# One attention and maxout FFN kernel: a new issue order, whole-row weight loads and two-bank folds

## The chip, the cores and the metric

The kernel runs on one core of a Trainium2 chip. The metric is device time in microseconds of one execution. The core has five engines that run side by side, each through its own queue in program order: TensorE (PE in the rows; its weight loads are PEld), VectorE (DVE), ScalarE (ACT), GpSimd (POOL) and SyncE (SP). POOL and SP issue the DMAs here. Engines wait for each other through semaphores.

## The reference

```python
a = softmax(phi)                       # over the 32 memory slots
k_m = einsum('bhsm,bhsd->bhmd', a, k)  # per head: 32 x 64
v_m = einsum('bhsm,bhsd->bhmd', a, v)
attn = softmax(q @ k_m.T / 8)          # 576 x 32 per head
x = attn @ v_m                         # heads side by side: 4608 x 512
h = maximum(maximum(x @ w1, x @ w2), x @ w3)   # 4608 x 768
out = h @ w_out                        # 4608 x 512, f32
```

Batch 8, heads 8, sequence 576, head size 64, 32 memory slots, d_ff 768. All inputs and the output are f32 in HBM; the loads cast to bf16, except phi.

## The kernel before

All heads of a batch are handled at once, in pairs of heads on 128 partitions. The program multiplies v_m into the weights instead of forming x: for each batch it makes "folded" weights v_m w1, v_m w2 and so on, and multiplies attn by those. The maximum over three is rewritten: with w1 and w2 replaced by w1 - w3 and w2 - w3 (w_diff, line 160), h is relu and max of two projections plus x w3, and the w3 part goes straight to the output through w3 w_out (made once by w3_t, line 137, and w3_o, line 148).

Work per batch b is cut into steps with letters (the table in issue, line 435). L loads phi, k, v and q. E is exp(phi) on ScalarE. B is k_m and v_m, 72 small matmuls into kvp. N normalizes on VectorE. K transposes k_m and v_m and VectorE copies them to kv and vk. Q0, Q1, Q2 transpose q, VectorE copies to qT. S0, S1 are the scores, then their exponentials on ScalarE (e2). M0, M1 are the sums over slots by a matmul with block ones and then, on ScalarE, logarithm and exponential, giving the reciprocal r. X0, X1 multiply e2 by r on VectorE into attn. D0, D1, D2 fold the weights, D3 folds w3 w_out; ScalarE evacuates even folds (line 344), VectorE odd ones (line 346). F0 to F11 are the projections: even ones end in a relu on ScalarE (h1, line 371), the odd one after it in a max with that h1 on VectorE (line 373) into hT. T0 to T3 are output tiles of 128 rows: six matmuls with w_out and two with the folded w3 part, a copy on ScalarE (line 417), and a store of two tiles on the SP queue. T4, of every second batch, is one more tile with the leftover 64 rows of two batches.

The order of all this is written out by hand as text (lines 461 to 485): each engine gets its instructions in the order in which the steps are issued. A plus or minus after a step's name means a later or an earlier batch. Batches 2 to 6 run in a loop, one pass each; a pass holds F and T of batch b, tiles T2, T3, T4 of batch b - 1, S to D of b + 1, B, N, K, Q and the loads further ahead.

PSUM is held as three buffers of two banks with the tag acc (kvp, sc, sm, wps, acc take turns) and two of one bank with the tag one (pt, kvt, po). A step waits until the reader of the tile three (or two) allocations earlier is done. phi, q, k and v have two buffers each, so loads run two batches ahead. All loads are issued by POOL, in program order: batch 0 in two halves, the weights in six pieces and w_out, then batch 1. Before the first data arrives, warm_up issues 16 matmuls on zeros.

Of the kernel before, what the change touches and what calls it, by code (L numbers as in the profile page):

```python
# [15 lines left out]
def kernel(  # L16
# [303 lines left out]
    def fold(b, n):  # L320

        s = st[b]
        W = BANK // 2
# [14 lines left out]
        if n < 3:  # L338
            out_ = wps[b][:, :, n].rearrange("p g i f -> p g (i f)")
        else:  # L340
            wp3s[b] = quad.tile([P, NG, DM], BF16, name="wp3")
            out_ = wp3s[b]
        if n % 2 == 0:
            nc.scalar.copy(out=out_, in_=ps)  # L344
        else:
            nc.vector.tensor_copy(out=out_, in_=ps)  # L346
# [35 lines left out]
    def ffn2(b, t):  # L382
# [31 lines left out]
        if t < 4:  # L414
            if t == 0:
                osts[b] = work.tile([P, 4, DM], FP32, name="ost")
            nc.scalar.copy(out=osts[b][:, t], in_=po)  # L417
            if t % 2 == 1:
# [14 lines left out]


    def issue(b, n):

        if not 0 <= b < B or (n == "T4" and b % 2 == 0):
# [14 lines left out]
            "T": lambda: ffn2(b, i),
        }[n[0]]()

    def run(b, text):

        for w in text.split():
            n = w.rstrip("+-")
            issue(b + w.count("+") - w.count("-"), n)

    warm_up(16)
    for h in range(2):
        att_exp(0, slice(2 * h, 2 * h + 2))
    for h in range(2):
        att_kv(0, range(2 * h, 2 * h + 2))
    run(0, "N Q0 Q1 Q2 L++ K S0 S1 M0 M1")
    w3_t(0)
    run(0, "X0 X1")
    w3_t(1)
    w3_t(2)  # L470
    for j in range(NP):
        w3_o(j)
    w_diff(0)
    run(0, "D0 D3 F0 F1 F2 F3")
    w_diff(1)
    run(0, "D1 F4 F5 E+")
    w_diff(2)
    run(0, "F6 F7 D2 F8 F9 F10 F11 T0 T1 B+ N+ T2 Q0+ Q1+ Q2+ K+ L+++ S0+ S1+")
# [37 lines left out]
```

## Time and profile before

| what | us |
|---|---|
| time before, median of 3 runs (218.95 to 221.14) | 220.83 |
| the profiled execution, its own time | 221.6 |
| span of that profile, first to last instruction | 219.8 |
| TensorE busy, VectorE busy, ScalarE busy, GpSimd busy | 182.0, 101.2, 107.2, 32.0 |
| mean granted clock of TensorE, as a share of full | 0.910 |

An engine's busy time is the sum of its instructions' records; a TensorE record includes its pipeline, so records of neighbours overlap, and the distance between two starts tells better what a step costs there. Idle time before an instruction is put down to the engine that released it. The span starts with the first instruction; the time of a run is some 2 us longer than the span.

### The profile page before, as it was taken

What the parts mean: (1) busy time and instruction counts of PE and PEld (TensorE: products, weight loads), DVE (VectorE), ACT (ScalarE), POOL (GpSimd) and SP (SyncE); (2) the same over time, 40 slices, a digit from 0 to 9 for tenths busy, and PEclk for the clock granted to TensorE, in tenths of its full rate; (3) what the DMA queues carried; (4) which work ended last, traced back from release to release, by engine and by line L of the source; (5) the groups of instructions that cost most, each with busy time, mean ns of one, the idle gap of its engine ahead of it and who ended that gap; (6) DMA issues with size and microseconds to landing.
All of it is one profiled execution on the core that took longest, in us unless ns stands there. A gap on an engine that the chain in (4) does not pass through costs nothing.

```text
span 219.8 us, 4458 instructions
## 1 busy us (share of the span) xinstructions
PE 182.0 (83%) x1912; PEld 100.7 (46%) x1912; DVE 101.2 (46%) x169; ACT 107.2 (49%) x178; POOL 32.0 (15%) x48
## 2 busy tenths in 40 slices
PE   7547896669787996499799988988998899899991
PEld 2234533335424743256345654564456445545540
DVE  6214705441608651942664295265525752552500
ACT  3102435343168439358265855674658259554431
POOL 8933230010401214120111110000000000000000
PEclk9855579679966999889999999999999999999998
DMA  4999999994796897999985994331033024113335
GB/s 99 187 204 207 202 262 208 263 207 137 136 210 170 179 206 160 232 219 207 211 175 160 142 204 74 98 98 35 13 98 95 4 47 102 57 37 95 98 95 143
DMA packets 23092, 31.75 MB, mean 144 GB/s; under 512 B 1312, under 2 KB 17440, under 8 KB 23072
## 3 DMA queue, kind: packets, MB, share of 16 engines
q0 software_dynamic: 17824, 22.02, 55.9%
q1 hardware_dynamic: 5248, 9.44, 16.1%
q8 instruction: 15, 0.25, 0.4%
q14 instruction: 5, 0.04, 0.1%
HBM read 39.32 MB, written 9.44 MB: 222 GB/s over the span
## 4 chain that ended last, share of the span: by engine, by line
PE 50%; ACT 19%; DVE 18%; issue 5%; DMA 5%; POOL 2%; ACTq 0%; DVEq 0%; POOLq 0%
PE po L388 19%; PE acc L361 13%; PE po L397 6%; DVE hT L373 6%; DMA qq<-in_q_dram 5%; ACT h L371 4%; ACT ln L300 4%; PE po L151 3%; PE wps L330 3%; ACT r L306 3%; DVE qT L241 3%; ACT ost L417 3%; ACT e L278 3%; DVE attn L311 3%; ACT wp L344 2%
## 5 line engine op out<-in xcount | busy, mean ns | idle before, releaser
L361 PE MATMUL acc<-attn,wp 128*128 128x288 bf16 x384 | 61.1, 304 | 5.5 <-ACT wp L344 1.7
L373 DVE TENSOR_TENSOR hT<-acc,h 128x576 bf16<-128x576 f32 x48 | 36.3, 756 | 48.3 <-ACT h L371 28.1
L388 PE MATMUL po<-wo_sb,hT 128*128 128x512 bf16 x216 | 55.1, 387 | 4.1 <-DVE hT L373 2.3
L361 PEld LDWEIGHTS <-wp 128*128 128x128 bf16 x384 | 38.2, 103 | 24.4 <-issue 6.2
L371 ACT ACTIVATE h<-acc 128x576 bf16<-128x576 f32 x48 | 30.6, 649 | 25.9 <-PE acc L361 25.7
L417 ACT COPY ost<-po 128x512 f32<-128x512 f32 x32 | 18.9, 590 | 41.4 <-PE po L397 41.4
L388 PEld LDWEIGHTS <-hT 128*128 128x128 bf16 x216 | 20.4, 99 | 30.8 <-issue 6.7
L346 DVE CAST wp<-wps 128x1024 bf16<-128x1024 f32 x16 | 19.1, 1221 | 19.6 <-PE wps L330 19.5
L397 PE MATMUL po<-wp,attn 128*128 128x512 bf16 x64 | 19.5, 387 | 0.0
L344 ACT CAST wp<-wps 128x1024 bf16<-128x1024 f32 x16 | 16.2, 1015 | 1.1 <-PE wps L330 1.1
L278 ACT ACTIVATE e<-sc 128x320 bf16<-128x320 f32 (+1 forms) x32 | 10.6, 425 | 12.6 <-PE sc L268 12.6
L311 DVE TENSOR_TENSOR attn<-e,r 128x576 bf16<-128x576 bf16 x16 | 12.0, 754 | 9.1 <-ACT r L306 9.0
L191 PE MATMUL kvp<-kvo,e 64*32 64x192 bf16 x576 | 9.7, 255 | 5.4 <-DMA kvo<-in_v_dram 4.5
L330 PE MATMUL wps<-w_sb,vk 64*32 64x512 bf16 x96 | 9.0, 391 | 5.3 <-DVE w_sb L164 3.0
L180 ACT ACTIVATE e<-ph 128x1152 bf16<-128x1152 f32 (+1 forms) x9 | 9.5, 1056 | 7.4 <-DMA ph<-in_phi_dram 7.4
L241 DVE COPY qT<-pt 128x1024 bf16<-128x1024 bf16 x16 | 10.8, 685 | 3.1 <-PE pt L238 2.9
L87 POOL DMA_DIRECT2D ph<-in_phi_dram x9 | 6.9, 762 | 36.5 <-ACT e L180 32.7
L191 PEld LDWEIGHTS <-e 64*32 64x32 bf16 x576 | 8.2, 94 | 7.1 <-issue 6.8
L238 PE MATMUL pt<-ident,qq 128*128 128x128 bf16 x128 | 10.3, 231 | 1.4 <-DMA qq<-in_q_dram 1.1
L306 ACT ACTIVATE r<-ln 128x576 f32<-128x576 f32 x16 | 10.9, 683 | 0.5
L300 ACT ACTIVATE ln<-sm 128x576 f32<-128x576 f32 x16 | 10.4, 650 | 0.1
L204 DVE RECIPROCAL rden<-kvp 128x2 f32<-128x2 f32 x8 | 1.3, 168 | 19.8 <-PE kvp L191 19.8
(50 smaller groups left out, 151.6 us busy)
## 6 DMA issues: line engine op xcount, KB each, us to landing
out_dram<-ost SPq DMA_DIRECT2D x32, 256.0 KB, 3.3
qq<-in_q_dram POOLq DMA_DIRECT2D x8, 576.0 KB, 9.3
ph<-in_phi_dram POOLq DMA_DIRECT2D x7, 576.0 KB, 9.2
kvo<-in_k_dram POOLq DMA_DIRECT2D x7, 576.0 KB, 8.6
kvo<-in_v_dram POOLq DMA_DIRECT2D x7, 576.0 KB, 11.3
w_sb<-in_moe_w_dram POOLq DMA_DIRECT2D x3, 512.0 KB, 17.7
out_dram<-ot SPq DMA_DIRECT2D x8, 128.0 KB, 2.4
w_sb<-in_moe_w_dram POOLq DMA_DIRECT2D x3, 256.0 KB, 16.3
```

What stands on the lines that cost most here:

```text
L191: nc.tensor.matmul(kvp[M * j : M * (j + 1), a, 0 : 3 * D], lhsT=s["e"][r, j, c, :], rhs=kv[r, :, j, c, :], start=(c == 0), stop=(c == NC - 1),
L300: nc.scalar.activation(out=ln.rearrange("p (h n) -> p h n", h=2), in_=sm[:, :, 0:SH], func=AF.Ln,)
L306: nc.scalar.activation(out=r, in_=ln, func=AF.Exp, scale=-1.0)
L311: nc.vector.tensor_tensor(out=attns[b // 2][:, g, (b % 2) * S : (b % 2 + 1) * S], in0=s["e2"][:, g, 0:S], in1=s["r", g], op=ALU.mult,)
L344: nc.scalar.copy(out=out_, in_=ps)
L346: nc.vector.tensor_copy(out=out_, in_=ps)
L361: nc.tensor.matmul(acc[:, h, 0:SH], lhsT=wps[b][:, g, ft // 2, w, (ft % 2) * P : (ft % 2 + 1) * P], rhs=attn[:, g, c0 : c0 + SH], start=(g ...
L371: nc.scalar.activation(out=s["h1"], in_=a, func=AF.Relu)
L373: nc.vector.tensor_tensor(out=hT[:, ft, (b % 2) * S : (b % 2 + 1) * S].rearrange("p (h n) -> p h n", h=2), in0=a, in1=s["h1"], op=ALU.max,)
L388: nc.tensor.matmul(po, lhsT=hT[:, fc, c0 : c0 + P], rhs=wo_sb[:, fc, :], start=(fc == 0), stop=False,)
L397: nc.tensor.matmul(po, lhsT=attn[:, g, c0 : c0 + P], rhs=wp3s[b][:, g, :], start=False, stop=(g == NG - 1),)
L417: nc.scalar.copy(out=osts[b][:, t], in_=po)
```

## The change

- The hand-written order is replaced by another, from the first load to the last tile. The prologue (batches 0 and 1 and the start of 2 and 3) is one list of steps with batch numbers; the loop text and the last batch's text are new. F's are no longer issued in pairs, output tiles no longer in the order 0 to 3, and D0 to D3 no longer side by side.
- Loads are split by tensor: load_ph, load_kv and load_q. In the main part each is issued as soon as its buffer's last reader has been issued (done), not all four after K. The first phi goes out on the SP queue, in two halves.
- w1, w2 and w3 come by one load each instead of two. w1 and w2 are treated as one row of 1536 columns (w12) and folded in three pieces of 512; w_diff works on the same pieces.
- The evacuations of D are ScalarE, VectorE, ScalarE, ScalarE (D3 was VectorE's), those of T are VectorE for T0, T1, T2 and T4 and ScalarE for T3 (all were ScalarE's).
- M is split: M issues the matmuls, R the logarithm and exponential.
- The warm-up is 28, 9 and 7 matmuls, at three places.

```diff
-    def load(b, parts=1):
+    def load_ph(b):
         ph = inp.tile([P, NP, NC, M], FP32, name="ph")
+        loaded.setdefault(b, {})["ph"] = ph
+        dst = ph.rearrange("p j c m -> p j (c m)")
+        if b == 0:
+            for h in halves:
+                nc.sync.dma_start(out=dst[:, h], in_=by_pair(phi, b)[:, h])
+        else:
+            nc.gpsimd.dma_start(out=dst, in_=by_pair(phi, b))
...
-    def load_w(i, cols):
+    def load_w(i):
         w = (moe_w1, moe_w2, moe_w3)[i]
         nc.gpsimd.dma_start(
-            out=w_sb[:, :, i, cols], in_=w.rearrange("(j p) f -> p j f", p=P)[:, :, cols]
+            out=w_sb[:, :, i], in_=w.rearrange("(j p) f -> p j f", p=P)
         )
 
-    load(0, 2)
+    load_ph(0)
+    load_kv(0)
+    load_q(0)
     ident = const.tile([P, P], BF16, name="ident")
     make_identity(nc, ident)
-    third = DF // 3
-    part = [slice(0, third), slice(third, DF)]
-    for h in range(2):
-        load_w(2, part[h])
+    load_w(2)
     nc.gpsimd.dma_start(out=wo_sb, in_=moe_w_out.rearrange("(t p) c -> p t c", p=P))
-    for h in range(2):
-        for i in range(2):
-            load_w(i, part[h])
-    load(1)
+    load_w(0)
+    load_w(1)
+    load_ph(1)
+    load_kv(1)
+    load_q(1)
...
+    EVAC = {"D": "avaa", "T": "vvvav"}
+
+    def evacuate(kind, n, out_, in_):
+        if EVAC[kind][n] == "a":
+            nc.scalar.copy(out=out_, in_=in_)
+        else:
+            nc.vector.tensor_copy(out=out_, in_=in_)
...
+    w12 = w_sb[:, :, 0:2].rearrange("p j i f -> p j (i f)")
+
     def w_diff(n):
 
-        c = slice(n * third, (n + 1) * third)
-        for i in range(2):
+        c = n * BANK
+        while c < (n + 1) * BANK:
+            e = min((n + 1) * BANK, (c // DF + 1) * DF)
             nc.vector.tensor_tensor(
-                out=w_sb[:, :, i, c],
-                in0=w_sb[:, :, i, c],
-                in1=w_sb[:, :, 2, c],
+                out=w12[:, :, c:e],
+                in0=w12[:, :, c:e],
+                in1=w_sb[:, :, 2, c % DF : c % DF + e - c],
                 op=ALU.subtract,
             )
+            c = e
...
-                    rhs=w_sb[r, j, 0:2, n * W : (n + 1) * W] if n < 3 else w3o[r, j, :],
+                    rhs=w12[r, j, n * BANK : (n + 1) * BANK] if n < 3 else w3o[r, j, :],
...
-                    lhsT=wps[b][:, g, ft // 2, w, (ft % 2) * P : (ft % 2 + 1) * P],
+                    lhsT=wps[b][:, g, w * DF + ft * P : w * DF + (ft + 1) * P],
...
+    issued = set()
+    loads = ((load_ph, "E"), (load_kv, "B"), (load_q, "Q0 Q1 Q2"))
...
+    def done(b, n):
+        issued.add((b, n))
+        for f, names in loads:
+            names = names.split()
+            if n in names and b + 2 < B and all((b, m) in issued for m in names):
+                f(b + 2)
...
+    issue(0, "Z28")
+    att_exp(0, halves[0])
+    att_exp(0, halves[1])
+    done(0, "E")
+    att_kv(0, range(0, NP // 2))
+    issue(0, "Z9")
+    att_kv(0, range(NP // 2, NP))
+    done(0, "B")
+    run(0, "N Z7 Q0 Q1 Q2 K S0 S1 W0 M0 R0 M1 R1")
+    for w in """
+        W1@0 W2@0 V0@0 O1@0 X1@0 X0@0 O2@0 O3@0 D0@0 V1@0 O0@0 V2@0 F2@0 D1@0
+        F0@0 D2@0 F10@0 F1@0 D3@0 F4@0 F3@0 E@1 F11@0 F8@0 F5@0 B@1 N@1 F9@0
+        K@1 F6@0 Q0@1 D3@1 Q2@1 F7@0 Q1@1 E@2 T1@0 S0@1 S1@1 D1@1 T0@0 M1@1
+        R1@1 T3@0 B@2 D0@1 M0@1 N@2 K@2 R0@1 Q0@2 D2@1 X0@1 D0@2 X1@1 E@3
+        D1@2 T2@0 F6@1 F0@1 Q1@2 F1@1 F10@1 F4@1 D3@2 F7@1 F2@1 Q2@2 F11@1 F5@1
+        F8@1 F3@1 S0@2 B@3 N@3 D2@2 S1@2 Q0@3 M0@2 Q2@3 R0@2 F9@1 Q1@3 M1@2
+        X0@2 T0@1 R1@2 X1@2 T1@1 K@3 E@4
+    """.split():
+        n, b = w.split("@")
+        issue(int(b), n)
     for b in range(2, B - 1):
-        run(b, "F0 F1 T2- S0+ S1+ B++ D0+ T3- N++ F2 M0+ F3 M1+ F4 X0+ F5 Q0++ X1+ F6 Q1++ F7 Q2++")
-        run(b, "T4- F8 F9 K++ L++++ F10 F11 E+++ T0 D1+ D2+ D3+ T1")
-    run(B - 1, "F0 F1 T2- F2 F3 F4 T3- F5 F6 F7 T4- F8 F9 F10 F11 T0 T1 T2 T3 T4")
+        run(b, "F0 F6 F1 F8 F4 F7 F2 F5 F10 F3 F9 T2- S0+ D1+ S1+ T3- Q0++ M0+ R0+")
+        run(b, "M1+ F11 Q1++ T0 R1+ T4- Q2++ E+++ D0+ X0+ B++ D3+ X1+ N++ D2+ T1 K++")
+    run(B - 1, "F0 F2 F3 F8 F1 T2- F10 F9 F4 T4- F6 F5 F11 F7 T3- T2 T4 T1 T0 T3")
```

W stands for w3_t, O for w3_o, V for w_diff, Z for warm_up.

## Rows read from the trace of the kernel before

**Rows 1.** The page: busy us, share of the span and count of each engine

```profile
PE 182.0 (83%) x1912; PEld 100.7 (46%) x1912; DVE 101.2 (46%) x169; ACT 107.2 (49%) x178; POOL 32.0 (15%) x48
```

**Rows 2.** Stage table: window, length, busy PE, PEld, DVE, ACT, POOL, clock, DMA, GB/s

```profile
0.00:45.00 45.00, 31.05 (x234) 16.61 (x234) 19.41 (x33) 13.43 (x21) 17.87 (x29) 0.73 1.12 204
...
92.50:116.10 23.60, 21.22 (x243) 11.94 (x239) 12.76 (x22) 12.59 (x21) 4.35 (x6) 0.95 1.06 208
116.10:135.80 19.70, 17.95 (x228) 10.56 (x226) 11.07 (x20) 12.50 (x21) 2.22 (x3) 1.00 0.81 148
135.80:158.10 22.30, 19.92 (x237) 11.36 (x236) 11.29 (x20) 13.08 (x22) 0.00 (x0) 1.00 0.25 60
...
178.00:196.60 18.60, 17.56 (x144) 9.05 (x143) 8.20 (x11) 11.91 (x21) 0.00 (x0) 1.00 0.30 72
196.60:219.80 23.20, 18.61 (x107) 9.93 (x105) 4.87 (x7) 8.39 (x14) 0.00 (x0) 0.96 0.41 102
```

**Rows 3.** Timeline, batch 3's pass and end of 6's: start, us, engine, line, tiles

```profile
118.75 0.32 PE L268 MATMUL sc<-qT,kv 64*32 64x320 bf16 x4
...
119.69 0.09 PEld L330 LDWEIGHTS <-vk 64*32 64x32 bf16 x1
...
122.67 0.41 PE L292 MATMUL sm<-e,blkones 128*128 128x288 bf16 x2
122.92 0.65 PE L361 MATMUL acc<-attn,wp 128*128 128x288 bf16 x4
123.68 0.76 DVE L373 TENSOR_TENSOR hT<-acc,h 128x576 bf16<-128x576 f32 x1 [2.84 <-PE acc L361]
...
125.09 0.61 PE L238 MATMUL pt<-ident,qq 128*128 128x128 bf16 x8
125.54 0.65 PE L361 MATMUL acc<-attn,wp 128*128 128x288 bf16 x4
...
133.28 0.39 PE L330 MATMUL wps<-w_sb,vk 64*32 64x512 bf16 x1
...
134.05 1.47 PE L388 MATMUL po<-wo_sb,hT 128*128 128x512 bf16 x6
135.79 1.14 PE L361 MATMUL acc<-attn,wp 128*128 128x288 bf16 x8
136.77 1.46 PE L388 MATMUL po<-wo_sb,hT 128*128 128x512 bf16 x6
...
188.21 1.46 PE L388 MATMUL po<-wo_sb,hT 128*128 128x512 bf16 x6
...
190.15 0.54 PE L361 MATMUL acc<-attn,wp 128*128 128x288 bf16 x3
```

**Rows 4.** The page's costliest groups: busy, mean ns, idle before and its releaser

```profile
L373 DVE TENSOR_TENSOR hT<-acc,h 128x576 bf16<-128x576 f32 x48 | 36.3, 756 | 48.3 <-ACT h L371 28.1
...
L371 ACT ACTIVATE h<-acc 128x576 bf16<-128x576 f32 x48 | 30.6, 649 | 25.9 <-PE acc L361 25.7
L417 ACT COPY ost<-po 128x512 f32<-128x512 f32 x32 | 18.9, 590 | 41.4 <-PE po L397 41.4
...
L346 DVE CAST wp<-wps 128x1024 bf16<-128x1024 f32 x16 | 19.1, 1221 | 19.6 <-PE wps L330 19.5
...
L344 ACT CAST wp<-wps 128x1024 bf16<-128x1024 f32 x16 | 16.2, 1015 | 1.1 <-PE wps L330 1.1
```

**Rows 5.** POOL's load issues in time; last, landing times of the q loads

```profile
24.55 0.74 POOL L87 DMA_DIRECT2D qq<-in_q_dram  x1 [3.07 <-DMA wo_sb<-in_moe_w_out_dram]
...
29.76 0.74 POOL L87 DMA_DIRECT2D kvo<-in_v_dram  x1 [1.53 <-DMA w_sb<-in_moe_w_dram]
32.57 0.74 POOL L87 DMA_DIRECT2D qq<-in_q_dram  x1 [2.07 <-DMA w_sb<-in_moe_w_dram]
...
DMA to landing us min/median/max: 6.1/9.3/19.3
```

**Rows 6.** Timeline of VectorE: the last difference of weights

```profile
43.87 1.28 DVE L164 TENSOR_TENSOR w_sb<-w_sb 128x1024 bf16<-128x1024 bf16 x2
```

More of the change, by code (lines that the diff above doesn't have):

```diff
@@ new lines, in load_kv, with load_q @@
+    def load_kv(b):
+        kv = kvos[b % 2]
+        loaded.setdefault(b, {})["kv"] = kv
+        for h in halves if b == 0 else [slice(0, NP)]:
+            for i, src in enumerate((k, v)):
+                nc.gpsimd.dma_start(
+                    out=kv[:, i].rearrange("p j c d -> p j (c d)")[:, h],
+                    in_=by_pair(src, b)[:, h],
+                )
+    def load_q(b):
+        qq = inp.tile([P, NP, NC, D], BF16, name="qq")
+        loaded.setdefault(b, {})["q"] = qq
+        nc.gpsimd.dma_start(
+            out=qq.rearrange("p j c d -> p j (c d)"), in_=by_pair(q, b)
+        )
@@ L229, in att_q @@
         qq = loaded[b]["q"]
-        if jj == 0:
+        if "qT" not in s:
             s["qT"] = work.tile([P, NP, NCP, P], BF16, name="qT")
@@ L257, in att_score @@
         x = b % 2
-        if g == 0:
+        if "e2" not in s:
             s["e2"] = work.tile([P, NG, S + HP], BF16, name="e2")
@@ L322, in fold @@
         s = st[b]
-        W = BANK // 2
-        if n == 0:
-            wps[b] = work.tile([P, NG, 3, 2, W], BF16, name="wp")
+        if n == 3:
+            wp3s[b] = quad.tile([P, NG, DM], BF16, name="wp3")
+        elif b not in wps:
+            wps[b] = work.tile([P, NG, 2 * DF], BF16, name="wp")
         ps = acc_pool.tile([P, NG, BANK], FP32, name="wps", tag="acc")
@@ L337, in fold @@
                 )
[L338 to L346, printed above, removed]
+        evacuate(
+            "D", n, wp3s[b] if n == 3 else wps[b][:, :, n * BANK : (n + 1) * BANK], ps
+        )
     hts = {}
@@ L353, in ffn1 @@
         ft, w = n // 2, n % 2
-        if n == 0 and b % 2 == 0:
+        if b // 2 not in hts:
             hts[b // 2] = work.tile([P, FT, 2 * S], BF16, name="hT")
@@ L369, in ffn1 @@
         if w == 0:
-            s["h1"] = quad.tile([P, 2, SH], BF16, name="h1")
-            nc.scalar.activation(out=s["h1"], in_=a, func=AF.Relu)
+            h1 = s["h1", ft] = quad.tile([P, 2, SH], BF16, name="h1")
+            nc.scalar.activation(out=h1, in_=a, func=AF.Relu)
         else:
@@ L414, in ffn2 @@
         if t < 4:
[L415 to L418, printed above, removed]
+            if b not in osts:
+                osts[b] = work.tile([P, 4, DM], FP32, name="ost"), set()
+            ost, done = osts[b]
+            evacuate("T", t, ost[:, t], po)
+            done.add(t)
+            t0 = t - t % 2
+            if {t0, t0 + 1} <= done:
                 rows = out[b * S : (b + 1) * S, :].rearrange("(p c) d -> p c d", c=NC)
                 for u in range(2):
-                    c0 = 2 * (t - 1) + (u + b) % 2
+                    c0 = 2 * t0 + (u + b) % 2
                     nc.sync.dma_start(
                         out=rows[:, c0 : c0 + 3 : 2, :],
-                        in_=osts[b][HP * u : HP * (u + 1), t - 1 : t + 1],
+                        in_=ost[HP * u : HP * (u + 1), t0 : t0 + 2],
                     )
@@ L427, in ffn2 @@
             ot = work.tile([P, DM], FP32, name="ot")
-            nc.scalar.copy(out=ot, in_=po)
+            evacuate("T", t, ot, po)
             for u in range(2):
@@ L440, in issue @@
         {
-            "L": lambda: load(b),
             "E": lambda: att_exp(b),
@@ L459, in run @@
[L459 to L478, printed above, removed]
@@ L479 @@
-    run(0, "T3 D0+ M0+ M1+ D1+ X0+ X1+ D2+ D3+ E++")
-    run(1, "F0 F1 F2 F3 B+ F4 F5 N+ F6 F7 Q0+ F8 Q1+ F9 Q2+ K+ L+++ F10 F11 T0")
-    run(1, "S0+ S1+ E++ D0+ T1 M0+ M1+ X0+ X1+ B++ D1+ D2+ N++ Q0++ Q1++ Q2++ K++ L++++ D3+ E+++")
+            issue(b + w.count("+") - w.count("-"), w.rstrip("+-"))
+    issue(0, "Z28")
[6 more added lines that the diff above has]
+    done(0, "B")
```

33 lines of the change are left out of this document (16 added, 17 removed).

## The prediction, made before the changed kernel was run

> **What bounds the kernel now.** I read the page's busy shares first, then a table by stage, then the instructions of one loop pass in order of time, then the load queue at the start. The shares say TensorE is busy 83% of the span, ScalarE 49%, VectorE 46% [rows 1]. That 83% overstates TensorE: its records overlap, so I use distances between starts. The stage table cuts the span at the first projection (F0) of each pass: 92.5 us until batch 2's pass begins, then 23.6, 19.7, 22.3, 19.9 and 18.6 us for the passes of batches 2 to 6 (the longer ones, those of even batches, carry a T4 output tile; the last has no B, K, Q or E left), and 23.2 us of tail [rows 2] (the pass of batch 5 is left out there, it repeats batch 3's). [...]
>
> What must TensorE spend on a pass at full clock? From starts [rows 3]: S and B together 0.94 (118.75 to 119.69), M 0.25, Q 0.45, three D 0.77, T 1.74 (134.05 to 135.79), F 0.49 (two in 0.98), T4 1.94. So 12 F 5.88 + 4 T 6.96 + S and B 0.94 + 4 D 1.1 + 2 M 0.5 + Q 1.2 + K 0.1 = 16.7 us, with T4 18.6. The passes take 19.7 and 22.3: **3.0 to 3.7 us of each pass are stalls**, and no engine is the bound. In the pass of batch 3 ScalarE is busy 12.5 us (6 h of 0.649, 4 tile evacuations of 0.59, two folds of 1.015, the rest exponentials and logarithms), VectorE 11.1 [rows 2, 4]. The stalls are waits in a fixed order with three PSUM buffers for acc: late in the pass D1, D2, D3 come back to back, ScalarE evacuates T's that the next h waits behind, and F's come in pairs of one ScalarE and one VectorE user, so each VectorE max waits for its own h.
>
> At the start the bound is loads and an order. DMA share is 1.12 over the first 45 us, above full by the way it is counted (overlapping packets) [rows 2]. The last weight half has landed at 32.57, when the queue's next issue is released by it; q of batch 1 is issued at 24.55 and the longest landing of a q load is 19.3 us, so it is there by about 43.9; q of batch 2, issued at 32.57, by 51.9 [rows 5]. But the third difference of weights runs only at 43.87, behind two VectorE max operations [rows 6], 11 us after its data.
>
> **The change, part by part.**
> *Weights and folds.* Six weight loads become three, same bytes; six differences of 1024 columns per partition become two of 2048 and two of 1024, the same total of 6144. Price nothing on bytes; w3's first transpose now waits for all of w3, but it runs behind the scores of batch 0 anyway. The differences are now at once behind the loads: V1's second piece about 0.65 after 32.6, V2 1.3 later, at 34.6 instead of 45.2. F's of batch 0 need D0, D1 and D2 earlier than before (all of w1's and w2's columns lie apart), so they begin in earnest at about 35.9 (D1's evacuation, 1.22, behind V2). *A new wait:* V0 stands on VectorE ahead of X1 and X0, and waits for the whole of w1, there by 29.7, when an issue is released by one of its halves [rows 5]; X1 and X0 (0.75 each, an estimate from VectorE's max) and the F's wait behind it. They end at about 32, still before V1's data: cost nothing while w2 lands at 32.5; if w2 came a microsecond earlier the cost would show.
>
> *First phi on SP.* It takes 0.75 us of issue twice off the POOL queue (an issue takes 0.74 [rows 5]), so k and v start 0.8 us sooner, yet they now share the engines with phi. Bounds: 1.5 gained, 1.5 lost; I take 0, since B's second half waits for the same total of bytes, and batch 1's q, 28 us later, sets the pace. [...]
>
> *Warm-up.* 16 matmuls become 28, 9 and 7. They fill time in which TensorE waits for loads; they may delay B's first half by under 1 us (an estimate from B's first half waiting for its data before too), which the second half of k and v covers. They may lift the clock for batch 0; I take nothing for it.
>
> *Loads.* Same bytes, each tensor issued once its last reader is issued, ph sooner than before. POOL holds kv behind ph's wait for E. B of batch 1 stands on TensorE ahead of F9, F6 and F7 of batch 0 and waits for v at about 40 (an estimate, one load ahead of q); Q0 waits for q at 43.9. 12 F's from 35.9 at about 0.6 each fill that time to 43, so little idles.
>
> *Evacuations.* 28 of 36 tile copies (T0, T1, T2, T4) go from ScalarE (0.59) to VectorE, 8 folds (D3) from VectorE (1.22) to ScalarE (1.015) [rows 4]. VectorE's price of a 128x512 fp32 copy isn't in the trace: from 0.756 for 576 and 1.221 for 1024 columns, 1.04 ns a column, it is 0.69; bounds 0.59 and 0.756. [...] Per pass ScalarE goes from 12.5 to 11.7 (three T less, one fold more), VectorE from 11.1 to 11.9, both under 16.7, so this is not on the path unless the order makes it so.
>
> *Order of a pass.* I walked the new order by hand, each queue in its own order, an engine reading a tile 0.2 us after TensorE has moved on (F at 122.92 takes 0.49, VectorE starts at 123.68, 0.27 later [rows 3]), buffers free 0.05 after a reader. Starts on TensorE from D0: B 0.2, D3 0.9, D2 1.6, T1 1.8, K 3.5, F0 3.6, F6 4.1, F1 4.6, F8 5.1, F4 5.6, F7 6.1, F2 6.6, F5 7.1, F10 7.6, F3 8.1, F9 8.6, T2 9.1, S0 10.8, D1 11.0, S1 11.2, T3 11.5, Q0 13.2, M0 13.7, M1 13.9, F11 14.2, Q1 14.6, T0 15.1, Q2 16.8, next D0 17.0. ScalarE then frees at 17.8, VectorE at 18.1, the state assumed at the first D0, so it repeats. D0 and D2 no longer stand together with D1; the T's give ScalarE time for its h's. With the starts' own spacing of rows 3 (some 0.3 more): 17.3, with T4 19.2; the pass of batch 6, without B, K and Q, about 17.1. Five passes: 19.2 + 17.3 + 19.2 + 17.3 + 17.1 = **90.1** against 104.1.
>
> *Until batch 2's F0.* From q of batch 1 at 43.9 TensorE still has Q, D3, F7 1.9; T's of batch 0 7.0; batch 1's S, M, three D, 12 F and two T 10.9; batch 2's B, K, Q, D, S, M 3.9; batch 3's B, Q, K 2.0: 25.7. The walk shows 2.6 of waits. 72.2; I add 1.8 for low clock behind the waits at 33 to 44 (bounds 0 and 4: half speed for up to 4 us of work). **74.0** against 92.5. *Tail:* the same 12 F and T's, last store a 256 KB one instead of 128 KB: **24.0** against 23.2.
>
> Sum: 74.0 + 90.1 + 24.0 = 188.1 of span. The profiled execution took 221.6 for a span of 219.8, so +1.8: 189.9; the runs shown have a median 0.8 below it, 220.83: **189 us**.
>
> **Rivals.**
> *A. Loads set the pace up to batch 3.* For: share 1.12 [rows 2], batch 2's q is there only by 51.9 [rows 5], while the walk wants B and Q of batch 2 at 51 to 53, and Q of batch 3 at 65 with the stores of batch 0 now in the way. Against: share falls to 0.25 once loads end, and a pass of 17 us is longer than a batch's loads. Price: 4 to 5 us late at batch 2 and again at batch 3, 9: 198.
> *B. The loop keeps its stalls.* The interleaving trades one buffer wait for another, e.g. VectorE at 11.9 of 17.3 is late for D1 and three T copies. Passes then keep 3.0 to 3.7 of stall, 14 us back: 203.
> *C. Walk too careful:* no stalls, first F0 at 70, passes 16.7 and 18.6: 181.
> [...]
>
> **How the numbers follow.** Forecast 0.58; A 0.18; B 0.12; C 0.07; D 0.05, of which 0.02 ends within 1%. A measurement of this kernel can't tell less than about 1% from no change. Range 181 to 200: it holds C, the forecast and A, 0.83; B and D stand outside. All cases but D are faster: 0.95, within 1% 0.02, slower 0.03.
>
> **What would show it.** F0 of batch 2 at 72 to 76; later passes at 17 to 19; V2 at 33 to 35; VectorE's copy of 512 at 0.69; ScalarE's h and VectorE's max with far fewer waits for each other. I am wrong if the loop's F0s stand 20 or more apart, if Q of batches 2 or 3 waits for a DMA for several us, if VectorE's queue makes TensorE wait for acc buffers, or if the clock column shows 0.5 beyond 45 us.

## The result, and the profile after

The changed kernel takes 186.09 us (median of 4 runs, 186.03 to 186.15) against 220.98 us (218.95 to 221.14) for the kernel before, run beside it: a ratio of 0.844, 95% interval 0.839 to 0.849. The profiled execution has a span of 184.2 us. I had forecast 189 with a range of 181 to 200. Single executions of the kernel before, and of kernels that keep its start, scatter by up to 5.5 us (216.29 to 221.76 over 17 of the kernel before), those of the changed kernel by 0.1, and why was not settled, so differences against the former hold to some 2 us.

First the page of the changed kernel: busy shares, and from the 40 slices the granted TensorE clock and the DMA share.

```profile
PE 170.7 (93%) x1940; PEld 97.8 (53%) x1940; DVE 110.1 (60%) x187; ACT 100.3 (54%) x158; POOL 28.3 (15%) x43
...
PEclk9999699999999999999999999999999999999996
DMA  5999999999999999998999699423021404240545
```

TensorE is busy 93% of a span that is 35.6 us shorter; before it was 83% [rows 1]. The clock (PEclk, in tenths; 9 is 0.9 or more) is up in all slices but one early one and the last.

Next the stage table of the changed kernel, cut at the first F0 of each pass as [rows 2] is (window, length, busy PE, PEld, DVE, ACT, POOL, clock, DMA share, GB/s).

```profile
0.00:68.96 68.96, 62.50 (x768) 34.56 (x769) 41.55 (x73) 37.36 (x57) 23.02 (x36) 0.98 1.13 227
68.96:88.20 19.24, 19.06 (x239) 11.44 (x237) 12.76 (x22) 12.08 (x19) 3.09 (x5) 1.00 1.11 247
88.20:105.72 17.52, 17.34 (x230) 10.64 (x228) 12.06 (x21) 12.04 (x19) 2.23 (x3) 1.00 0.98 208
105.72:124.96 19.24, 19.06 (x240) 11.44 (x238) 12.75 (x22) 12.09 (x19) 0.00 (x0) 1.00 0.75 152
124.96:142.47 17.51, 17.33 (x229) 10.62 (x227) 12.06 (x21) 11.03 (x18) 0.00 (x0) 1.00 0.25 62
142.47:159.40 16.93, 16.93 (x146) 9.20 (x144) 10.46 (x16) 10.08 (x18) 0.00 (x0) 1.00 0.29 71
159.40:184.20 24.80, 18.45 (x107) 9.94 (x105) 8.46 (x12) 5.57 (x9) 0.00 (x0) 0.93 0.40 102
```

The reader is to see three things. Until batch 2's F0 it takes 68.96 us, 23.5 less than before. The five passes take 159.40 - 68.96 = 90.4 us, 13.7 less, and within each TensorE's busy time is at most 0.2 us short of the pass: next to nothing is left to wait for. The tail is 1.6 longer. 23.5 + 13.7 - 1.6 = 35.6, the whole difference of the spans. Of the start's 23.5, 17.4 is idle time of TensorE (23.9 before, 6.5 now) and 6.1 its busy time (68.6 and 62.5), at a granted clock of 0.81 before and 0.98 now.

The groups that answer to [rows 4] (busy, mean ns of one | idle before and its releaser):

```profile
L397 DVE TENSOR_TENSOR hT<-acc,h 128x576 bf16<-128x576 f32 x48 | 35.5, 755 | 17.2 <-PE acc L385 16.0
L395 ACT ACTIVATE h<-acc 128x576 bf16<-128x576 f32 x48 | 29.7, 651 | 19.2 <-PE acc L385 19.2
L154 DVE COPY ost<-po 128x512 f32<-128x512 f32 x24 | 16.6, 691 | 19.2 <-PE po L421 19.2
```

VectorE's max used to stand idle 28.1 us for ScalarE's relu [rows 4]; now it, the relu and the tile copies all wait for TensorE.

At the start, POOL's loads (start us, us, line, what ended the idle time before), VectorE's differences of weights, and from TensorE the first F after all folds, the weight load that begins Q0 of batch 1, and Q0 of batch 3:

```profile
7.06 1.61 POOL L113 DMA_DIRECT2D w_sb<-in_moe_w_dram  x2
...
15.06 0.74 POOL L107 DMA_DIRECT2D qq<-in_q_dram  x1 [2.09 <-DMA qq<-in_q_dram]
...
29.86 1.83 DVE L187 TENSOR_TENSOR w_sb<-w_sb 128x1024 bf16<-128x1024 bf16 x2 [0.52 <-DMA w_sb<-in_moe_w_dram]
...
32.88 1.15 PE L385 MATMUL acc<-attn,wp 128*128 128x288 bf16 x8 [0.73 <-DVE wp L154]
...
39.80 0.45 PEld L262 LDWEIGHTS <-qq 128*128 128x128 bf16 x8 [0.37 <-DMA qq<-in_q_dram]
...
63.06 0.62 PE L262 MATMUL pt<-ident,qq 128*128 128x128 bf16 x8 [1.06 <-DMA qq<-in_q_dram]
```

The last differences run the moment w2 is there, at 29.86, and the F's run from 32.88. Q0 of batch 1 starts at 39.80; its q was issued at 15.06 and its landing, in the trace, is 24.7 later, at 39.76. The weight load waits 0.37 for it, but the matmuls before it end only at 39.73: TensorE itself stands idle for under 0.1 us there. From there to 62.00 its gaps sum to 0.3 us; the next wait is the 1.06 us for q of batch 3, which is issued at 42.44, behind the Q's of batch 1 that read the same buffer.

### The profile page after: what moved, and what is told of

Same layout as the page of the kernel before. It is cut to its first block, busy times and chain, and to the rows that moved or that the text cites. A ratio compares the mean times of both kernels' runs of the same rounds, so it can differ in the third digit from the quotient of the medians.

```text
span 184.2 us, 4510 instructions
## 1 busy us (share of the span) xinstructions
PE 170.7 (93%) x1940; PEld 97.8 (53%) x1940; DVE 110.1 (60%) x187; ACT 100.3 (54%) x158; POOL 28.3 (15%) x43
## 4 chain that ended last, share of the span: by engine, by line
PE 61%; DMA 23%; ACT 4%; POOL 4%; issue 3%; DVE 2%; POOLq 0%
PE po L412 22%; PE acc L385 22%; DMA w_sb<-in_moe_w_dram 12%; DMA qq<-in_q_dram 11%; PE po L421 6%; PE wps L360 3%; PE pt L262 2%; ACT wp L152 2%; POOL kvo L99 2%; PE sm L316 1%; PE po L430 1%; PE sc L292 1%; DVE w_sb L187 1%; POOL w_sb L113 1%; ACT r L335 1%
## 5 line engine op out<-in xcount | busy, mean ns | idle before, releaser
L385 PE MATMUL acc<-attn,wp 128*128 128x288 bf16 x384 | 52.5, 286 | 0.7 <-DVE wp L154 0.7
L412 PE MATMUL po<-wo_sb,hT 128*128 128x512 bf16 x216 | 52.6, 380 | 0.0
L385 PEld LDWEIGHTS <-wp 128*128 128x128 bf16 x384 | 36.5, 98 | 13.2 <-DVE wp L154 1.0
L395 ACT ACTIVATE h<-acc 128x576 bf16<-128x576 f32 x48 | 29.7, 651 | 19.2 <-PE acc L385 19.2
L412 PEld LDWEIGHTS <-hT 128*128 128x128 bf16 x216 | 19.8, 98 | 23.9 <-issue 3.8
L154 DVE COPY ost<-po 128x512 f32<-128x512 f32 x24 | 16.6, 691 | 19.2 <-PE po L421 19.2
L152 ACT CAST wp<-wps 128x1024 bf16<-128x1024 f32 x24 | 23.4, 1014 | 7.9 <-PE wps L360 7.9
L143 PE MATMUL po<-warm 128*128 128x512 bf16 x44 | 12.6, 450 | 1.2 <-DVE warm L131 1.2
L152 ACT COPY ost<-po 128x512 f32<-128x512 f32 x8 | 4.7, 586 | 15.3 <-PE po L421 15.3
L107 POOL DMA_DIRECT2D qq<-in_q_dram x8 | 6.0, 744 | 43.1 <-PE pt L271 33.0
L329 ACT ACTIVATE ln<-sm 128x576 f32<-128x576 f32 x16 | 10.3, 645 | 2.2 <-PE sm L316 1.8
L421 PEld LDWEIGHTS <-attn 128*128 128x128 bf16 x64 | 6.3, 98 | 7.4
L262 PEld LDWEIGHTS <-qq 128*128 128x128 bf16 x128 | 8.2, 98 | 3.2 <-DMA qq<-in_q_dram 1.6
## 6 DMA issues: line engine op xcount, KB each, us to landing
kvo<-in_k_dram POOLq DMA_DIRECT2D x7, 576.0 KB, 17.5
```

The source lines that it names most:

```text
L143: nc.tensor.matmul(po[:, 0:BANK], lhsT=warm[:, 0:P], rhs=warm, start=True, stop=True)
L152: nc.scalar.copy(out=out_, in_=in_)
L154: nc.vector.tensor_copy(out=out_, in_=in_)
L262: nc.tensor.transpose(pt[:, i, c, :], qq[:, 2 * jj + i, 2 * c : 2 * c + 2, :], ident)
L385: nc.tensor.matmul(acc[:, h, 0:SH], lhsT=wps[b][:, g, w * DF + ft * P : w * DF + (ft + 1) * P], rhs=attn[:, g, c0 : c0 + SH], start=(g == ...
L395: nc.scalar.activation(out=h1, in_=a, func=AF.Relu)
```

## The experiments

The theory that I went in with: three things make the gain. The order of the passes takes their stalls away (not the new split of the copies); the order of the start keeps TensorE fed while loads arrive; the loads set when the start can go, by q of batch 1. Rivals: the split of the copies makes the passes; or the loads make the start by themselves. "After" is the changed kernel, 186.09.

**1. The old split of copies in the new order.**

```diff
-    EVAC = {"D": "avaa", "T": "vvvav"}
+    EVAC = {"D": "avav", "T": "aaaaa"}
```

> The changed kernel with the old split of evacuations alone: D3 back on VectorE, all output tiles T back on ScalarE. Theory (the order makes the gain of the loop, the split only helps): a pass gives ScalarE back three tile copies of 0.59 and takes one fold of 1.015 away, so about 0.8 us more of ScalarE work per pass; passes lengthen by 0.3 to 0.8 us from 17.5 and 19.2, the whole by 2 to 5 us: 188 to 191 us. Rival (the split of evacuations makes the gain): passes go back towards 19.7 and 22.3, the whole to 198 us or more.

193.86 us (192.94 to 194.70), 7.8 slower: between both. The passes take 20.16, 21.28, 20.19, 18.54 and 16.93. ScalarE and TensorE in the second pass (start, us, [idle before and its releaser]):

```profile
104.50 0.58 ACT L152 COPY ost<-po 128x512 f32<-128x512 f32 x1 [1.54 <-DMA out_dram<-ost]
104.98 0.66 ACT L329 ACTIVATE ln<-sm 128x576 f32<-128x576 f32 x1
105.67 0.68 ACT L335 ACTIVATE r<-ln 128x576 f32<-128x576 f32 x1
106.25 1.15 ACT L204 ACTIVATE e<-ph 128x1152 bf16<-128x1152 f32 x1
107.31 0.99 ACT L152 CAST wp<-wps 128x1024 bf16<-128x1024 f32 x1
...
108.35 0.37 PE L360 MATMUL wps<-w_sb,vk 64*32 64x512 bf16 x1 [2.25 <-ACT wp L152]
108.69 2.65 PE L412 MATMUL po<-wo_sb,hT 128*128 128x512 bf16 x6
```

T0's copy, now ScalarE's, stands in its queue ahead of R1, E and D0's evacuation. ScalarE stands idle 1.54 us until T0 is computed (the row names a store, but T0's last matmuls, at 103.86 for 0.59, end just before the copy starts), and the evacuation that D2 waits for comes at 107.31: TensorE is idle 2.25 us. In the four full passes it waits 5.7 us for this evacuation. Then six matmuls of T1 take 2.65 instead of 1.46: the granted clock of 105 to 111 is 0.82, and 0.50 from 109 to 112. With ScalarE busy 12.86 us of this pass's 21.28, it is a place in a queue that costs, not ScalarE's load: some 1 us in three passes, 3.8 in this one, and 2.0 ahead of batch 2's F0 (8.6 in this execution). T's copies and D3's fold were put back together; neither was tried alone.

**2. The old order of the passes, all else as changed.**

```diff
-        run(b, "F0 F6 F1 F8 F4 F7 F2 F5 F10 F3 F9 T2- S0+ D1+ S1+ T3- Q0++ M0+ R0+")
-        run(b, "M1+ F11 Q1++ T0 R1+ T4- Q2++ E+++ D0+ X0+ B++ D3+ X1+ N++ D2+ T1 K++")
-    run(B - 1, "F0 F2 F3 F8 F1 T2- F10 F9 F4 T4- F6 F5 F11 F7 T3- T2 T4 T1 T0 T3")
+        run(b, "F0 F1 T2- S0+ S1+ B++ D0+ T3- N++ F2 M0+ R0+ F3 M1+ R1+ F4 X0+ F5 Q0++ X1+ F6 Q1++ F7 Q2++")
+        run(b, "T4- F8 F9 K++ F10 F11 E+++ T0 D1+ D2+ D3+ T1")
+    run(B - 1, "F0 F1 T2- F2 F3 F4 T3- F5 F6 F7 T4- F8 F9 F10 F11 T0 T1 T2 T3 T4")
```

> The changed kernel with the old order of steps in the passes of batches 2 to 6 and in the last batch, everything else as changed. Theory (order makes the gain of the loop): the first F0 of batch 2 stays at 69 us, the passes go back to 19 to 22 us, less at most 1 us each because the tile copies no longer hold ScalarE: 194 to 199 us. Rival (evacuations make it): 187 to 189 us.

196.36 us (196.18 to 196.57), as the theory has it. Stage table:

```profile
0.00:68.94 68.94, 61.56 (x768) 34.68 (x769) 41.55 (x73) 37.45 (x57) 23.01 (x36) 0.98 1.14 229
68.94:91.07 22.13, 19.91 (x239) 11.37 (x237) 13.62 (x25) 11.73 (x19) 3.09 (x5) 1.00 1.17 253
91.07:110.89 19.82, 18.23 (x229) 10.82 (x228) 12.06 (x21) 11.96 (x20) 2.22 (x3) 1.00 1.04 213
```

The start is untouched. The passes take 22.1, 19.8, 22.1, 19.7 and 18.4, within 0.3 us of those before the change wherever the clock was full there [rows 2], although the tile copies are on VectorE: the split is worth next to nothing in the old order, and by (1) 1 to 3.8 us in each full pass of the new. The five passes and the tail together are 10.3 us longer than after, the difference of the medians.

What TensorE waits for in the five passes, before and then after (who waited for whom, total us, times, longest):

```profile
PE pt L247 <- DVE qT L241: 3.0, 4, 0.7
PE po L388 <- DVE hT L373: 2.1, 4, 0.6
PE po L388 <- DVE qT L241: 1.8, 2, 0.9
```

```profile
PE wps L360 <- ACT wp L152: 0.7, 4, 0.2
```

In (2) the same three waits stand again with the same 3.0, 2.1 and 1.8. So in the old order TensorE waits mostly for VectorE, whose copies of qT and max operations stand in one queue. Waits for a reader of an acc buffer (h, e) sum to 1.4 of 8.3 before.

**3. Only the passes: the kernel before with the new order of passes and the new split.** (Its start and loads are untouched; the steps R and the helper for copies are carried over, and the helper moves the copies of the start too.)

```diff
+    EVAC = {"D": "avaa", "T": "vvvav"}
...
-        run(b, "F0 F1 T2- S0+ S1+ B++ D0+ T3- N++ F2 M0+ F3 M1+ F4 X0+ F5 Q0++ X1+ F6 Q1++ F7 Q2++")
-        run(b, "T4- F8 F9 K++ L++++ F10 F11 E+++ T0 D1+ D2+ D3+ T1")
+        run(b, "F0 F6 F1 F8 F4 F7 F2 F5 F10 F3 F9 T2- S0+ D1+ S1+ T3- Q0++ M0+ R0+")
+        run(b, "M1+ F11 Q1++ T0 R1+ T4- Q2++ E+++ D0+ X0+ B++ D3+ X1+ N++ D2+ T1 K++ L++++")
```

> The kernel before with the new order of the passes of batches 2 to 6 and of the last batch and the new split of evacuations; its loads, weights, warm-up and its order up to batch 2 stay. Theory (start and loop are independent gains): F0 of batch 2 at about 92, then passes of 17.5 and 19.2 and a tail of 24.8: 207 to 210 us, and what this saves and what the run with the old passes loses add up to the whole. Rival (the loop needs the early loads of the new start): passes stay above 19, 213 us or more.

209.06 us (205.48 to 210.38), in the range expected, 11 to 12 below the kernel before run beside it. That this gain and the loss of (2), 10.3, would add up to the whole was a slip: both measure the same part, the passes, and agree. Its first pass, from 91.19, still takes 21.28 at a clock of 0.92; the later ones are, to the hundredth, those of the changed kernel:

```profile
112.47:129.99 17.52, 17.34 (x228) 10.63 (x227) 12.07 (x22) 12.03 (x19) 2.79 (x4) 1.00 0.94 197
129.99:149.23 19.24, 19.06 (x238) 11.44 (x237) 12.75 (x23) 12.08 (x19) 0.00 (x0) 1.00 0.80 156
```

So of 35 us about 10 to 12 belong to the passes and their order, and 23 to 25 to the start.

**4. The old order of the start, with the new loads, folds, copies and passes, and the old warm-up.**

```diff
-    for w in """
-        W1@0 W2@0 V0@0 O1@0 X1@0 X0@0 O2@0 O3@0 D0@0 V1@0 O0@0 V2@0 F2@0 D1@0
-        F0@0 D2@0 F10@0 F1@0 D3@0 F4@0 F3@0 E@1 F11@0 F8@0 F5@0 B@1 N@1 F9@0
-        K@1 F6@0 Q0@1 D3@1 Q2@1 F7@0 Q1@1 E@2 T1@0 S0@1 S1@1 D1@1 T0@0 M1@1
...
+    run(0, "N Q0 Q1 Q2 K S0 S1 M0 R0 M1 R1 W0 X0 X1 W1 W2 O0 O1 O2 O3")
+    run(0, "V0 D0 D3 V1 V2 D1 D2 F0 F1 F2 F3 F4 F5 E+")
+    run(0, "F6 F7 F8 F9 F10 F11 T0 T1 B+ N+ T2 Q0+ Q1+ Q2+ K+ S0+ S1+")
+    run(0, "T3 D0+ M0+ R0+ M1+ R1+ D1+ X0+ X1+ D2+ D3+ E++")
+    run(1, "F0 F1 F2 F3 B+ F4 F5 N+ F6 F7 Q0+ F8 Q1+ F9 Q2+ K+ F10 F11 T0")
+    run(1, "S0+ S1+ E++ D0+ T1 M0+ R0+ M1+ R1+ X0+ X1+ B++ D1+ D2+ N++ Q0++ Q1++ Q2++ K++ D3+ E+++")
```

> The changed kernel (its loads, copies, passes and last batch) with the order of the start as before the change: batch 0's F's in pairs and all twelve ahead of batch 1's B, 16 warm-ups, V1 and V2 together behind D0 and D3. Theory: the old order costs batches 0 and 1 about what it costs a pass of the loop, 3 to 5 us each, and the loads give the rest of the 25 us that the start has gained: first F0 of batch 2 at 75 to 80, total 192 to 197. Rival: the order of the start is nearly all of the gain, whatever the loads do: first F0 at 85 or later, 202 or more.

200.28 us (197.84 to 202.34): 14.2 slower than after, between theory and rival. In the profiled execution, whose span of 195.9 belongs to the shortest of these times, batch 2's F0 stands at 79.31, inside what the theory gave. Stage table:

```profile
0.00:79.31 79.31, 61.07 (x735) 34.34 (x740) 42.70 (x76) 34.76 (x55) 22.30 (x35) 0.91 1.12 223
79.31:99.89 20.58, 20.25 (x241) 12.06 (x237) 11.73 (x20) 14.05 (x21) 3.78 (x6) 0.93 0.64 131
99.89:117.41 17.52, 17.19 (x226) 10.63 (x227) 12.07 (x21) 12.04 (x19) 2.22 (x3) 1.00 0.98 211
```

And TensorE's waits between 28 and 92 us (who waited for whom, total us, times, longest):

```profile
PE pt L271 <- DVE qT L265: 2.6, 1, 2.6
PE wps L360 <- ACT ln L329: 1.5, 2, 0.8
PE kvp L215 <- ACT wp L152: 0.7, 1, 0.7
```

These, the largest of 9.1 us of such waits (2.9 in after), are for evacuations and VectorE's copies, such as the old start had. Behind them the first pass of the new loop takes 20.58 at a clock of 0.93, against 19.24 at 1.00. So the order of the start is worth 11.7 (this execution) to 14 us (medians), and what is left of the start's 23, some 9 to 12, comes with the rest: the changed loads and folds, and V1 and V2 ahead of the F's. How it divides among these was not measured.

**5. Only the loads: the kernel before with whole-row weight loads and the first phi on SP.**

```diff
+            eng = nc.sync if src is phi and b == 0 else nc.gpsimd
...
-    for h in range(2):
-        for i in range(2):
-            load_w(i, part[h])
+    load_w(0, slice(0, DF))
+    load_w(1, slice(0, DF))
```

> The kernel before the change, its order untouched, with whole-row weight loads and batch 0's phi on the SP queue. Theory: its third weight difference stands behind VectorE's max operations at 43.9 us whatever the loads do, so that earlier weights are worth little without the order: 217.5 to 220.5. Rival: the loads alone bring much of the start: 215 or less.

219.35 us (217.74 to 220.60) beside 219.72 for the kernel before; the 95% interval of the ratio is 0.999 to 1.009. The theory holds; the loads bring nothing by themselves. VectorE's rows say why:

```profile
30.08 0.69 DVE L163 TENSOR_TENSOR w_sb<-w_sb 128x1024 bf16<-128x1024 bf16 x1 [3.02 <-DMA w_sb<-in_moe_w_dram]
36.73 1.28 DVE L163 TENSOR_TENSOR w_sb<-w_sb 128x1024 bf16<-128x1024 bf16 x2
42.72 1.28 DVE L163 TENSOR_TENSOR w_sb<-w_sb 128x1024 bf16<-128x1024 bf16 x2
```

All weights are there by about 30, yet the last differences run at 42.72 with no wait for a DMA, behind VectorE's own queue, 1.15 earlier than before [rows 6]. So earlier loads are worth nothing in the old order. In the new one the old ways of loading, put back one at a time, cost 1.4, 0.5 and 0.3 us (6, 7, 10): most of the start's gain is the order, the place of V1 and V2 included. The new order with all of the old loads was not run, nor was the place of V1 and V2 tried alone.

**6. The first phi on POOL, as before.**

```diff
-                nc.sync.dma_start(out=dst[:, h], in_=by_pair(phi, b)[:, h])
...
+            if b == 0:
+                nc.gpsimd.dma_start(
+                    out=loaded[0]["ph"].rearrange("p j c m -> p j (c m)")[:, h],
+                    in_=by_pair(phi, b)[:, h],
+                )
```

> The changed kernel with the first phi on the POOL queue, in halves ahead of each half of k and v, as before the change. Theory (phi on SP saves the two issues of 0.75 us at the head of the POOL queue): q of batch 0 is in 0.8 us later (15.8 instead of 15.0) and everything behind it too: 186.7 to 187.2 us. Rival (the same 16 engines move the same bytes, the sum does not change): 186.0 to 186.3 us.

187.50 us (187.12 to 187.81): 1.4 slower, above what I expected. The rows that answer to those of after:

```profile
8.57 0.78 POOL L117 DMA_DIRECT2D w_sb<-in_moe_w_dram  x1
...
16.23 0.74 POOL L111 DMA_DIRECT2D qq<-in_q_dram  x1 [2.10 <-DMA qq<-in_q_dram]
...
31.79 1.83 DVE L191 TENSOR_TENSOR w_sb<-w_sb 128x1024 bf16<-128x1024 bf16 x2 [0.61 <-DMA w_sb<-in_moe_w_dram]
...
41.74 0.45 PEld L266 LDWEIGHTS <-qq 128*128 128x128 bf16 x8 [0.38 <-DMA qq<-in_q_dram]
```

Two issues more in POOL's queue push the weights' issues by 1.5 us (w1 at 8.57 against 7.06), the last weight comes 1.9 later and q of batch 1 too (41.74 against 39.80). In the first 10 us the DMA engines move 138 GB/s instead of 162, at a share of 0.75 instead of 0.88. Early on POOL alone does not issue loads fast enough to fill them; with the SP queue beside it they fill sooner, and 40 us later the lost time is still missing. Whether SP's queue also moves the same two loads faster was not tested; the 1.5 us of issue leave 0.4 of the 1.9 open.

**7 and 8. The weight loads in halves: by columns (rows of 1 and 2 KB, as before) and by rows (rows stay whole).**

```diff
+        for cols in (slice(0, DF // 3), slice(DF // 3, DF)):
...
+                in_=w.rearrange("(j p) f -> p j f", p=P)[:, :, cols],
```

```diff
+        for h in halves:
+            nc.gpsimd.dma_start(
+                out=w_sb[:, h, i], in_=w.rearrange("(j p) f -> p j f", p=P)[:, h]
```

> The changed kernel with w1, w2 and w3 loaded in two column pieces each (256 and 512 columns, rows of 1 and 2 KB instead of 3 KB), order w3, w_out, w1, w2. Theory (whole rows move faster): w3 took 4.0 us behind q instead of 4.9 before, w1 and w2 together 6.9 instead of 8.0; so the last weight lands about 2 us later, at 31.5 to 32, and as loads follow each other without a gap up to batch 3 the whole is 1.5 to 2.5 us longer: 187.5 to 188.5 us. Rival (row length does not matter, the loads came sooner for another reason): 186.0 to 186.5 us.

> The changed kernel with each of the three weights in two loads of half the rows (rows stay whole, 3 KB); as many loads as in the run with half columns. Theory (row length): lands as in the changed kernel, 186.0 to 186.5 us. Rival (number of loads, through the queue's limit of loads in flight): 187.5 us or more, like half columns.

186.57 (186.24 to 187.02) and 186.17 us (185.96 to 186.71). The theory of (7) is a miss: the last difference does not wait for its data, F's begin at 32.95 against 32.88, and the whole is 0.5 longer, not 1.5 to 2.5. Twice the weight loads cost nothing (8); shorter rows cost 0.4 to 0.5 by the medians, though the single runs of (7) and (8) overlap. What (7) loses is lost at batch 1: TensorE waits 0.72 us for its v and 0.16 for its q. In both, q of batch 1 is issued at 23.02 and 22.44 instead of 15.06 and lands at 40.7 and 40.2 instead of 39.8 (landing times 17.7 and 17.8): an issue 7 to 8 us earlier moves the landing by 0.5 to 1 us. With the DMA share at 1.15 or more from 10 to 40 us in all three, the bytes ahead of this load set its landing here, not its issue.

In the profiled execution of (8) the granted clock (third value from the end) is below full once more after the F's begin, 0.50 from 33 to 36 us (eight matmuls of F from 32.81 take 2.10 us, in after 1.15):

```profile
30.00:40.00 10.00, 8.55 (x132) 4.86 (x131) 6.23 (x10) 5.70 (x8) 1.81 (x3) 0.83 1.19 236
```

**9. Sixteen warm-ups as before instead of 28, 9 and 7.**

```diff
-    issue(0, "Z28")
+    issue(0, "Z16")
...
-    issue(0, "Z9")
...
-    run(0, "N Z7 Q0 Q1 Q2 K S0 S1 W0 M0 R0 M1 R1")
+    run(0, "N Q0 Q1 Q2 K S0 S1 W0 M0 R0 M1 R1")
```

> The changed kernel with the old warm-up alone: 16 matmuls at the start, none between the halves of B and before Q0. Theory (the fillers hold the clock): the granted clock falls to 0.5 from about 10 us as it did before, the 24 matmuls of w3_o take up to 10 us instead of 5, the F's of batch 0 come 2 to 3 us later, part of it covered by the later loads: 187 to 189 us. Rival (loads set the pace anyway): 186.0 to 186.5 us with a clock column of 0.5 up to 25 us.

186.03 us (185.91 to 186.39): the rival. The clock (third value from the end) falls in the second ten microseconds, and nothing follows from it: the F's begin at 32.81, against 32.88 in after, since they wait for the weights:

```profile
10.00:20.00 10.00, 6.63 (x84) 4.85 (x85) 3.46 (x10) 1.27 (x4) 2.97 (x4) 0.56 1.19 204
20.00:30.00 10.00, 8.41 (x55) 4.60 (x55) 5.26 (x8) 6.15 (x11) 1.48 (x2) 0.92 1.15 238
30.00:40.00 10.00, 8.15 (x138) 4.72 (x137) 7.57 (x13) 6.06 (x9) 2.97 (x4) 1.00 1.19 237
```

**10. Loads of a batch issued behind K of the batch two earlier, not each behind its own last reader.**

```diff
-    loads = ((load_ph, "E"), (load_kv, "B"), (load_q, "Q0 Q1 Q2"))
+    loads = ((load_ph, "K"), (load_kv, "K"), (load_q, "K Q0 Q1 Q2"))
```

> The changed kernel, but the loads of phi, k and v of batch b+2 wait until K of batch b is issued, instead of following the last reader of each tensor. Theory: the loads of batches 1 and 2 are queued on the POOL queue behind the weights anyway, and only batch 3's are late, by the 3 to 5 us that lie between E and K of batch 1; the one wait left in the changed kernel for a load (Q0 of batch 3, 1.06 us) grows by at most that: 186.5 to 189. Rival: issuing each tensor at its own last reader is a large part of the start's gain: 190 or more, with B or Q of batches 2 and 3 waiting for loads for 4 us and more in sum.

186.40 us (186.05 to 186.53): 0.3 above after, a hair under the theory's range; Q0 of batch 3 waits 0.82 us, no longer than in after. k of batch 3 is issued at 38.48 against 38.40: POOL waits for the reader of k's buffer anyway.

**11 and 12. Searching for more.** First three moves at once: E behind F9, T4 last in the last batch, T0 of batch 1 ahead of Q0 of batch 3. Then T4 last, and D2 behind T1 in each pass.

```diff
-        run(b, "M1+ F11 Q1++ T0 R1+ T4- Q2++ E+++ D0+ X0+ B++ D3+ X1+ N++ D2+ T1 K++")
-    run(B - 1, "F0 F2 F3 F8 F1 T2- F10 F9 F4 T4- F6 F5 F11 F7 T3- T2 T4 T1 T0 T3")
+        run(b, "M1+ F11 Q1++ T0 R1+ T4- Q2++ E+++ D0+ X0+ B++ D3+ X1+ N++ T1 D2+ K++")
+    run(B - 1, "F0 F2 F3 F8 F1 T2- F10 F9 F4 T4- F6 F5 F11 F7 T3- T2 T3 T1 T0 T4")
```

> The changed kernel with three moves: in a pass E goes from before D0 to after F9, where ScalarE idles 2.35 us while T2 runs; in the last batch T4 is the last tile in place of T3; before batch 2, T0 of batch 1 goes ahead of Q0 of batch 3, which waits 1.06 us for its load. Theory: D2 no longer waits 0.37 us per pass for the buffer of D0 (1.9 us in five passes), the store at the end is 128 KB pieces again (1 to 1.7 us), the load's wait is covered (1 us): 181.5 to 183.5 us. Rival (the moved E is late at its load or holds the scores' exponentials): 186 us or more.

> The changed kernel with two moves: T4 last in the last batch (its store is 128 KB, T3's pair 256 KB) and, in each pass, D2 of the next batch behind T1 instead of ahead of it. Theory: D2 waits 0.37 us a pass for ScalarE's evacuation of D0, and T1 fills that wait; T4 last shortens the tail by 1.3. 1.3 plus up to 1.8: 183.0 to 184.8. Rival: T1 ahead of D2 only moves the wait (VectorE's copies of T0 and T1 come closer, or D2's evacuation is late for F7): 184.6 to 185.2, passes unchanged at 17.5 and 19.2.

187.05 (186.70 to 187.54) and 185.56 us (185.37 to 185.70). The first is a miss by 3.5 or more: the tail is 1.3 shorter as expected, but the passes stay at 17.5 and 19.2, and batch 2's F's come some 2.3 later: the wait for q of batch 3 is gone, and in its place TensorE waits for VectorE, 0.74 us for attn and 1.4 in four places before it. The second is the fastest kernel here, 0.5 under after, yet above the ranges of both theory and rival: the tail gives 1.1, and 0.3 are lost in the pass of batch 6 and 0.4 ahead of batch 2's F0, where nothing was changed. D2's wait for ScalarE is gone, but it was 0.18 us a pass in after and not the 0.37 that I had priced, and the full passes are within 0.14 of the old ones:

```profile
69.36:88.46 19.10, 18.94 (x237) 11.35 (x237) 13.12 (x23) 11.17 (x18) 3.01 (x5) 1.00 1.09 238
88.46:105.95 17.49, 17.33 (x226) 10.53 (x227) 12.07 (x22) 12.04 (x19) 2.31 (x4) 1.00 1.00 210
...
159.91:183.60 23.69, 18.54 (x112) 10.01 (x106) 8.23 (x12) 5.77 (x9) 0.00 (x0) 0.96 0.42 105
```

## Why the prediction was right, step by step

- **Passes.** 90.1 forecast, 90.4 measured, and one by one 19.2, 17.3, 19.2, 17.3, 17.1 against 19.24, 17.52, 19.24, 17.51, 16.93. The cause named was the order, and (2) and (3) show it. Of the waits named within it, the acc buffers and the T's on ScalarE that the next h waits behind were not the ones that held TensorE: they were for VectorE's qT and hT, and stayed the same when (2) took the T's off ScalarE. The bound of 16.7 that I gave TensorE was too low: a pass without waits has 17.3 us of it (S and B take 1.1, not 0.94, since 119.69 was the weight load of D0, which runs ahead of its matmuls, at 120.11; an F takes 0.51, not 0.49). So the old passes held some 2.4 to 3.2 us of stall, not 3.0 to 3.7; the 17.3 of the forecast came from adding 0.3 to the walk's 17.0. Rival C was never open in the passes, and (11) and (12) found nothing more there. Rival B (stalls stay) is out by the same rows, rival D, a low clock that lasts into the loop, by the clock of 1.00 in every pass.
- **Copies.** VectorE's price of 0.69 was right (691 ns). "Not on the path unless the order makes it so" holds, with (1) showing such an order: the copy's cost is not its 0.59 or 0.69 but what stands behind it while it waits. The move of the T's to VectorE, together with D3's to ScalarE, was worth 7.8 us in the new order.
- **Start: the mis-sized term, 69.0 instead of 74.0.** The step was "q of batch 1 sets the pace". It does so only in a tie with the weights: the F's keep TensorE busy from 32.88 (I had 35.9) to 39.73, and q is in at 39.76. A later v and q cost time, as (7) shows (F0 at 69.72 instead of 68.96); what an earlier q alone would gain was not tried, and here it would have found TensorE still at its F's. From its landing to batch 2's F0 I had 25.7 + 2.6 + 1.8 = 30.1; measured 68.96 - 39.76 = 29.2, and it is much the same in three variants (28.9 in 6, 29.0 in 7, 28.9 in 8). That this sum comes out is in part luck: TensorE's work in it is 28.1 and not 25.7, its waits 1.1 and not 2.6, and the 1.8 for a low clock did not come. The anchor was off by 4.1 of the 5.0: I took 24.55 plus the longest landing of any q load, 19.3. The trace of before had this load's own landing, 17.4, so 41.95, which would have taken off 1.9. The other 2.2 are the loads' own gain (41.95 to 39.76), which I had priced at nothing: phi on SP 1.9 of it (6).
- **Phi on SP, priced 0 with bounds of 1.5 either way.** Worth 1.4. I had written both halves of the answer: two issues of 0.75 off POOL's queue, and loads that set the pace. The 1.5 us that they take from the issuing queue, while it does not keep the engines full (a DMA share of 0.75 in the first 10 us, 0.88 without them), come back as 1.9 us at the weights and at q of batch 1 (6). My 0 rested on the same total of bytes and left this out.
- **Low clock, priced 1.8.** The 1.8 was an estimate; the trace of before shows a clock of 0.66 from 40 to 45 us and 0.71 from 45 to 50, with idle times of TensorE of 2.24, 1.36, 0.80 and 1.14 us from 37 to 47. None in the profiled execution of after: 1.00 from 30 us on. That is no property of the order: in (8), which keeps it, the clock is 0.50 from 33 to 36 us, and batch 2's F0 still comes only 0.14 later, with no wait for q of batch 3 left. So a low clock there is mostly hidden by that wait for a load, a slack that the sum did not have.
- **V0 ahead of X1 and X0.** It cost the weights nothing, as worked out: in the trace X1 and X0 end at 28.7, and w2's difference still waits 0.52 for its data, at 29.86. The differences end at 31.7; I had 34.6.
- **Rival A, loads set the pace up to batch 3.** Half true: the DMA share stays above 1.1 until batch 3's pass, but only one wait for them is left after the weights, 1.06 us before Q0 of batch 3 (its q took 20.6 us to land).
- **Warm-up and whole rows, priced 0.** Under 0.1 (9) and 0.4 to 0.5 (7 against 8 and after), neither clear of the spread of the runs.
- **Tail.** 24.0 forecast, 24.8 measured; T3's pair as the last store costs 1.1 to 1.3, as (11) and (12) show.

## What to carry to other kernels

Where no engine is full and the waits are between neighbours in hand-written queues, walk the order queue by queue: a step's cost is what stands behind it while it waits (a copy of 0.58 us, and TensorE idle for 2.25: 1), and what a split of work between engines is worth goes by the order (7.8 us in the new, next to nothing in the old: 1, 2). Earlier data pay only if the order lets the first reader run (219.35 us with them in the old order, 219.72 without: 5), so do not judge a change of loads in the old order. Before naming a cause, look up what the engine on the path waits for: the longest idle times here stood on other engines (48.3 us of VectorE, 41.4 of ScalarE [rows 4]). For a load in a full queue reckon from when its own bytes landed, not from its issue plus the longest landing of its kind: moved from 24.55 to 15.06, the q load landed 2.2 us sooner, not 9.5.
